# Exponentials written over their tile's scores: one place of two banks each for scores and exponentials becomes two places that hold both

## The chip, the cores and the metric

The kernel runs on one core of one Trainium2 chip. The metric is the device time of one execution in microseconds; lower is better. Five engines matter: TensorE (PE, matrix products, with its weight loads shown as PEld), VectorE (DVE), ScalarE (ACT), GpSimd (POOL) and SyncE (SP, which issues the transfers). Each engine takes its instructions in the order in which the program was written out for it, and waits at an instruction until what that needs is there. The products of PE land in PSUM, eight banks of 2 KB for each of the 128 partitions.

## The reference, cut to what matters

Attention that keeps the 32 largest scores of each row, for 8 batches, 8 heads, 576 positions and 64 columns for each head, and behind it a two-layer network with a rational function between its layers.

```python
def _attn_ref(q, k, v):
    scores = scale * np.matmul(q, k.transpose(0, 1, 3, 2))
    kth = np.partition(scores, -top_k, axis=-1)[..., -top_k:-top_k + 1]
    scores = np.where(scores >= kth, scores, -1000000000.0)
    scores = scores - np.max(scores, axis=-1, keepdims=True)
    attn = np.exp(scores)
    attn = attn / (np.sum(attn, axis=-1, keepdims=True) + 1e-09)
    return np.matmul(attn, v).astype(np.float32)

def _moe_ref(x, w_in, w_out, a, b):
    h = x @ w_in
    h2 = h * h
    h3 = h2 * h
    P = a[0] + a[1] * h + a[2] * h2 + a[3] * h3
    Q = 1.0 + np.abs(b[0]) * np.abs(h) + np.abs(b[1]) * h2
    return ((P / (Q + 1e-06)) @ w_out).astype(np.float32)
```

x has 4608 rows of 512; the hidden layer is 2048 wide.

## The kernel before

**Tiles.** A tile is 128 rows of queries of one head against all 576 keys: 288 tiles, 32 of which hold the 64 left-over rows of two heads (`mixed`). For one tile the steps are, with their lines:

- PE makes the scores (`s`, line 719, or 716 for a mixed tile) in two banks of PSUM; ACT copies them to SBUF (`sb`, 726).
- DVE looks for the 32nd largest score. The 576 columns are three thirds. Four *folds* (745) compare thirds in pairs: the first two take `s` and `sb` and give the smaller and the larger (into `pr`), the other two take `s` and the larger (into `x` and `pr`). Two searches (751) take the eight best of what was folded away. Then four searches for the eight best (762, into `m`) alternate with three *strike-outs* (770) of the eight just found. This is a chain; only the folds and the two searches of 751 have some freedom.
- POOL makes the negative maximum (`st`, 287), ACT the exponentials (`e`, 824), which read `sb` and are written to two other banks of PSUM.
- DVE makes the *masked sum* (827): it compares `sb` with the 32nd value, multiplies with `e`, writes `pr`, and sums.
- PE transposes `pr` (`trp`, 925 and 933), ACT copies the transposes (`p`, 944), and PE multiplies with the values (`av`, 958), for two or four tiles at once and in three parts, on half of the array's columns at a time (128*64 in the trace).

**Hidden layer.** When eight such units have made 256 columns of x (a chunk; 18 in all), PE runs eight groups of hidden products (`ph`, 1116: each of three passes of high and low parts), ACT and POOL the rational function, and PE the output products (`po`, 1311, for the first chunk 1304). The last chunk runs after the last tile. The weights come as float64 and are turned to float32 at the start by ACT, DVE and POOL (512 to 540), and split in high and low parts (565 to 572). The constants of the rational function (`co`, 315 to 430) are worked out on POOL.

**What sets the order.** `add` lists every step with its engine, length, inputs and a due time (`key`); `Plan.run` walks through time and lets each engine take the ready step with the smallest due time, and writes its instructions out there and then. So the order on every engine follows from the table `KEY` (line 21). A `Hold` is a place in a ring (`room`, 223): a step with `take` cannot be chosen while all places of that tag are taken, and the last of the steps with `give` frees it. PSUM's eight banks are: `s` one place of two banks, `e` one place of two banks, `mm` two of one bank (hidden products, transposes, value products), `o` two of one bank (output). Scores hold `s` until the copy and the four folds are through (five users); exponentials hold `e` until the masked sum. `UK` in `KEY` sets how soon the first and the last fold (`f0`, `f3`) come, `AV` how soon the value products come.

Of the kernel before, what the change touches and what calls it, by code (L numbers as in the profile page):

```python
# [20 lines left out]
KEY = {'XM': 1, 'LN': 12, 'UV': 'DVE', 'UK': -883.243, 'B0': ('ACT',), 'B1': ('POOL', 'DVE'), 'B2': ('DVE', 'POOL'), 'B3': ('DVE', 'POOL'), 'WH': ('POOL', 'ACT'), 'XH': ('POOL', 'ACT'), 'TH': 0, 'EU': -3.981, 'HW': 256, 'Q0': ('POOL', 'ACT'), 'Q1': ('POOL',), 'SPLIT': (0, 1, 2, 3, 4, 5, 6, 7), 'XS': 1, 'RH': ('ACT',), 'p2': ('POOL',), 'p4': ('POOL',), 'ratio': ('POOL',), 'ratio_low': ('POOL',), 'URG': -41.622, 'PT': -20.047, 'AV': -43.299, 'MOE': 39.596, 'LOOK': 0.253, 'T': 5.414, 'KL': 0.37, 'PJ': 24.436, 'WL': -1.095, 'EX': 21.72, 'EW': 13.405, 'ALT': {'ACT': 0.627, 'DVE': 84.969, 'POOL': 10.704}, 'WG': 7.127, 'QL': -9.213, 'PACE': 11.13, 'MS': -4.816, 'NM': ('POOL',), 'WD': ('POOL', 'ACT'), 'LP': ('POOL',), 'VL': 2.562, 'VF': 9.72, 'KF': -73.607, 'KG': 4.863, 'PG': 19.476, 'LS': 14.977, 'LG': 7.167, 'PE0': (), 'PO0': 1, 'OK': -24.113, 'OG': 9.815, 'MB': 2, 'KM': 2.703, 'QF': -0.407, 'CUB': (), 'SOFT': 1.0, 'RA': ('POOL', 'ACT'), 'CK': 3.655, 'CO': -111.173, 'CA': -110.941, 'OB': 1, 'CD': 2.11, 'CF': 99.691, 'PL': 0}  # L21
# [15 lines left out]
class Plan:  # L37
# [11 lines left out]
    BACK = 0.17  # L49

    def __init__(self, room):
        self.ring = {t: [-1.0] * n for t, n in room.items()}
        self.left = dict(room)
        self.steps = []
    def fits(self, take):
# [12 lines left out]
    def add(self, eng, length, emit, after=(), key=0.0, take=(), give=(), crit=False, alt=1.0, behind=(), soft=0.0):  # L68
# [8 lines left out]
        s.sig = tuple(sorted(need.items()))  # L77
# [12 lines left out]
        return s  # L90

    def run(self):
# [12 lines left out]
        while left:  # L105
# [9 lines left out]
            while again:  # L115
                again = False
                for e in engines:
# [15 lines left out]
                    again = True  # L133
                    s.end = now + s.length
# [19 lines left out]
    def choose(self, e, ready, soon, now):  # L154
        tops = []
        for sig, q in ready.items():
            while q and q[0][2].end is not None:
                heapq.heappop(q)
            if q:
                tops.append((q[0][0], q[0][1], sig))  # L160
# [22 lines left out]
def tile_topk_attention__then__rational_ffn(  # L183
# [13 lines left out]
    P = 128  # L197
# [272 lines left out]
    def weight_block(name, key, after):  # L470
# [21 lines left out]
        turn, xhold = [] if inner else [Hold("wt")], Hold("mm")  # L492
# [52 lines left out]
        for i in range(len(parts)):  # L545
            s = add("ACT", act_sb(n) + 0.0004 * n, low(i), [ld, s], key + 1,
                    take=([xhold, *hold] if inner else [xhold]) if i == 0 else [])
            d = add("DVE", dve(n), high(i), [s], key + 1)
            signs.append(add("ACT", act_sb(n), sign(i), [d], key + 1))
# [148 lines left out]
    def add_tile(t):  # L698
        t.probs = t.ex = None
        u, kv, key = t.u, t.u.kv, t.key  # L700
        shold = Hold("s", 3 if full or KEY["UV"] == "POOL" else 5)
# [6 lines left out]
        hihold, ehold = Hold("hi") if full else u.xhold, Hold("e")  # L708
# [108 lines left out]
        def exps():  # L817
# [5 lines left out]
            t.e = bank("e", [P, 2, 512], f"e_{t.nm}")[:, :, 0:HF]  # L823
# [21 lines left out]
        else:  # L845
# [12 lines left out]
        ex = add("ACT", act_sb(S, 1), exps, [nm_, u.tiles[0].ex], key + KEY['EX'],  # L858
                 take=[ehold] + (([u.phold, u.uhold] if full else [u.uhold]) if t.h == 0 else []))
# [30 lines left out]
    def add_values(u):  # L890
# [133 lines left out]
        for cs in cuts:  # L1024
            m = add("PE", cold(u.tiles[0].n) * len(cs) * n_av, multiply(cs), [m] if m else pair.ev + [pair.vload], key + KEY['AV'],
                    take=[] if m else [avh] + ([] if u.chunk.parts or u.mixed else [u.chunk.hold]))
# [65 lines left out]
    def add_group(x, o, g, key, split, xs, oholds):  # L1092
# [9 lines left out]
        mm, th = Hold("mm"), {n: Hold("t") for n in ("h", "va", "hh", "pa", "g", "gl")}  # L1102

        def hidden(f, c):
            def emit():
                if f == 0 and c == 0:
                    y.ph = bank("mm", [P, 512], f"ph_{nm}")
# [126 lines left out]
        for f in range(FG):  # L1234
# [11 lines left out]
        if not full:  # L1246
            mm.users = 3
            e1 = add("ACT", act(512, 1), moved, [last, prev.e], ku, give=[mm], take=fours[0:3])
# [122 lines left out]
    def build():  # L1371
# [66 lines left out]
        if not full:  # L1438
# [7 lines left out]
            for _ in range(7):  # L1446
                s = add("POOL", 6 * 0.18, slope_of_root, [s], key=KEY['CD'])
                s = add("DVE", 0.08, turned_slope, [s], key=KEY['CD'])
                s = add("POOL", 0.36, next_root, [s], key=KEY['CD'])
            s = add("POOL", 0.54, near_root, [s], key=KEY['CD'])  # L1450
            for _ in range(2):
                s = add("POOL", 10 * 0.18, slope_near, [s], key=KEY['CD'])
                s = add("DVE", 0.08, turned_slope, [s], key=KEY['CD'])
# [129 lines left out]
```

## Time and profile before

| | us |
|---|---|
| median of 3 runs (1491.86 to 1493.81) | 1493.15 |
| the profiled execution | 1492.21 |
| its span, first to last instruction | 1490.3 |
| PE busy | 1397.2 |
| DVE busy | 1331.9 |
| ACT busy | 1325.9 |
| POOL busy | 1220.5 |

The profile is of one execution. A row of a timeline gives start, length and engine, then line, operation, output<-input, shape and count. A PE instruction's length overlaps the next one's, and a DVE instruction's too by a little, so that the pace of an engine is read from start to start. The span's last 100 us hold no attention.

### The profile page before, as it was taken

The numbers are of one execution on the slowest core, as the hardware profiler recorded it, in microseconds if no ns is written. First come the engines' busy times: TensorE is split into PE (matmuls) and PEld (weight loads), VectorE is DVE, ScalarE is ACT, GpSimd is POOL, SyncE is SP. The second block draws the span as 40 slices with busy tenths as digits, with TensorE's granted clock in tenths as the row PEclk, the third lists the DMA queues.
The fourth block names the chain that finished last, engine by engine and source line by source line (L and its number), as shares of the span: only waits on it lengthen the run. The fifth ranks groups of instructions, "written<-read, shape, count | busy, mean of one in ns | idle before, by whom it ended". The sixth has DMA issues, their size and how long they took to land.

```text
span 1490.3 us, 32446 instructions
## 1 busy us (share of the span) xinstructions
PE 1397.2 (94%) x9793; PEld 1169.7 (78%) x9793; DVE 1331.9 (89%) x5418; ACT 1325.9 (89%) x2440; POOL 1220.5 (82%) x1908
## 2 busy tenths in 40 slices
PE   2657999999999999999999999999999999999997
PEld 1335677888888888888888888888888888888886
DVE  6899999999999999999989998999999999999200
ACT  7898879999898989999899999999899989999785
POOL 8898889779876798779887888779877888777785
PEclk9857999999999999999999999999999999999999
DMA  6764466234533255333533354334533345332333
GB/s 243 254 228 146 135 202 205 86 103 118 165 111 114 89 153 156 90 111 116 172 109 105 98 152 149 103 92 127 173 114 89 118 134 166 89 111 68 100 101 100
DMA packets 110824, 197.25 MB, mean 132 GB/s; under 512 B 15664, under 2 KB 32048, under 8 KB 110640
## 3 DMA queue, kind: packets, MB, share of 16 engines
q1 hardware_dynamic: 110640, 195.08, 43.2%
q8 instruction: 80, 1.31, 0.4%
q14 instruction: 104, 0.85, 0.2%
HBM read 167.78 MB, written 14.68 MB: 122 GB/s over the span
## 4 chain that ended last, share of the span: by engine, by line
PE 72%; ACT 9%; DVE 9%; POOL 5%; DMA 3%; issue 2%; SPq 0%; POOLq 0%; ACTq 0%; DVEq 0%
PE ph_m L1116 19%; PE po_m L1311 17%; PE av L958 9%; PE s L719 7%; PE trp L925 7%; PE po_t L1311 3%; PE ph_t L1116 3%; PE s L716 2%; DVE m L762 2%; DVE pr L827 1%; ACT e L824 1%; PE po_m L1304 1%; DVE pr L745 1%; DVE x L770 1%; DMA w_wo<-in_moe_w_out_dram 1%
## 5 line engine op out<-in xcount | busy, mean ns | idle before, releaser
L1116 PE MATMUL ph_m<-xh_m,win 128*128 128x256 f32 x2048 | 432.9, 289 | 3.7 <-ACT p L944 3.3
L1116 PEld LDWEIGHTS ph_m<-xh_m,win 128*128 128x128 f32 x2048 | 336.8, 188 | 15.3 <-ACT p L944 5.7
L762 DVE MAX8 m<-x 128x8 f32<-128x192 f32 (+1 forms) x864 | 309.4, 358 | 3.8
L1116 PE MATMUL ph_m<-xl_m,win 128*128 128x256 f32 x1024 | 286.1, 279 | 0.0
L925 PE MATMUL trp<-ident,pr 128*128 128x128 f32 x1312 | 226.9, 283 | 38.9 <-ACT wout L535 11.6
L944 ACT COPY p<-trp 128x512 f32<-128x512 f32 (+1 forms) x448 | 229.4, 514 | 22.8 <-PE trp L925 11.6
L719 PE MATMUL s<-k,q 128*128 128x288 f32 x1024 | 201.0, 320 | 37.0 <-DVE x L745 21.6
L827 DVE SCALAR_TENSOR_TENSOR pr<-sb,m,e 128x576 f32<-128x576 f32 x288 | 230.5, 800 | 3.5 <-ACT e L824 2.1
L824 ACT ACTIVATE e<-sb,st 128x576 f32<-128x576 f32 x288 | 217.7, 756 | 17.5 <-POOL st L287 8.6
L925 PEld LDWEIGHTS trp<-ident,pr 128*128 128x128 f32 x1312 | 161.9, 144 | 81.6 <-ACT wout L535 17.8
L745 DVE TENSOR_TENSOR pr<-s,sb 128x192 f32<-128x192 f32 x576 | 198.1, 347 | 25.6 <-ACT sb L726 24.5
L726 ACT COPY sb<-s 128x576 f32<-128x576 f32 x288 | 185.9, 646 | 37.6 <-PE s L719 27.8
L1175 POOL TENSOR_TENSOR pa_m<-pa_m,va_m 128x512 f32<-128x512 f32 x128 | 165.5, 1293 | 54.7 <-ACT va_m L1172 53.4
L719 PEld LDWEIGHTS s<-k,q 128*128 128x128 f32 x1024 | 155.9, 198 | 66.4 <-POOL k L622 10.7
L1311 PE MATMUL po_m<-wout,g_m 128*128 128x512 f32 x480 | 201.9, 421 | 0.0
L751 DVE MAX8 x<-pr 128x8 f32<-128x192 f32 x576 | 199.3, 346 | 0.0
L770 DVE MATCH_REPLACE8 x<-m,x 128x192 f32<-128x192 f32 x576 | 198.3, 344 | 0.0
L1116 PEld LDWEIGHTS ph_m<-xl_m,win 128*128 128x128 f32 x1024 | 193.3, 189 | 3.1 <-issue 0.5
L1311 PE MATMUL po_m<-wl_m,g_m 128*128 128x512 f32 x480 | 189.9, 396 | 1.7 <-DMA wl_m<-wout_l 1.7
L1311 PE MATMUL po_m<-wout,gl_m 128*128 128x512 f32 x480 | 189.4, 395 | 1.9 <-POOL gl_m L1190 1.8
L958 PE MATMUL av<-p,vm 128*64 128x256 f32 (+1 forms) x1920 | 185.2, 341 | 1.6 <-ACT p L944 1.6
L1141 POOL TENSOR_TENSOR pa_m<-pa_m,hh_m 128x512 f32<-128x512 f32 x128 | 165.6, 1294 | 13.7 <-ACT pa_m L1181 4.7
(129 smaller groups left out, 3235.3 us busy)
## 6 DMA issues: line engine op xcount, KB each, us to landing
wl_m<-wout_l SPq DMA_DIRECT2D x240, 256.0 KB, 2.7
vm<-in_v_dram SPq DMA_DIRECT2D x96, 320.0 KB, 3.0
kx<-in_qk_dram SPq DMA_DIRECT2D x64, 288.0 KB, 3.1
qx<-in_qk_dram SPq DMA_DIRECT2D x64, 256.0 KB, 3.0
km<-in_qk_dram SPq DMA_DIRECT2D x32, 352.0 KB, 3.6
w_wo<-in_moe_w_out_dram SPq DMA_DIRECT2D x32, 256.0 KB, 4.8
win<-in_moe_w_in_dram SPq DMA_DIRECT2D x16, 512.0 KB, 5.6
out_dram<-ob_m SPq DMA_DIRECT2D x32, 256.0 KB, 3.4
```

The source lines that it names most:

```text
L719: nc.tensor.matmul(s[:, hf, 0:HF], u.pair.q.q[:, i, t.h, o : o + P], kv.k[:, t.h, cols], start=(i == 0), stop=(i == 1),)
L745: engine().tensor_tensor(out=to, in0=one_, in1=two_, op=op)
L751: nc.vector.max(t.x[:, o : o + 8], t.w[:, 2 * i * TH :][:, 0:TH])
L762: nc.vector.max(t.m[:, 8 * r : 8 * r + 8], src)
L770: nc.vector.match_replace(y, t.m[:, 8 * r : 8 * r + 8], x, NEG)
L824: nc.scalar.activation(t.e, t.sb, AF.Exp, scale=SCALE, bias=t.st)
L827: nc.vector.scalar_tensor_tensor(out=t.pr, in0=t.sb, scalar=t.kth, in1=t.e, op0=ALU.is_ge, op1=ALU.mult, accum_out=u.ss[:, t.h : t.h + 1],)
L925: nc.tensor.transpose(u.ps[i][:, c * P : (c + 1) * P], u.pr[:, x], ident)
L944: nc.scalar.copy(pair.pT[i][:, at].rearrange("p c n -> p (c n)")[:, 0:nw], u.ps[i][:, 0:nw])
L958: nc.tensor.matmul(pair.av[d, 0 : u.nq * len(pair.units)], lhs, x[:, 0, d] if u.mixed else x[:, 0] if lone else x, start=(c == 0), stop=(c ...
L1116: nc.tensor.matmul(y.ph[:, f * nt : (f + 1) * nt], w[c, ff][:, at : at + P], z[:, c, :], start=(c == 0 and i == 0), stop=(c == HP - 1 and ...
L1311: nc.tensor.matmul(o.po[i], z, w, start=(ff == 0 and n == 0), stop=(ff == NF - 1 and n == 2),)
```

## The change

The room for `e` goes, and `s` has two places of two banks. The exponentials of a tile are written over its scores, in the same banks, so a place is held from the scores to the masked sum (six users instead of five), and the exponentials have the four folds among the steps they come after. In a tile's terms: the scores of tile n+1 no longer wait for the folds of tile n, those of tile n+2 wait for the masked sum of tile n.

```diff
     room = KEY.get('ROOM') or {
-        "s": 1, "e": 1, "mm": 2, "o": 2,
+        "s": 2 if KEY["EI"] else 1, "e": 0 if KEY["EI"] else 1, "mm": 2, "o": 2,
...
-        shold = Hold("s", 3 if full or KEY["UV"] == "POOL" else 5)
+        shold = Hold("s", (3 if full or KEY["UV"] == "POOL" else 5) + KEY["EI"])
...
-        hihold, ehold = Hold("hi") if full else u.xhold, Hold("e")
+        hihold, ehold = Hold("hi") if full else u.xhold, shold if KEY["EI"] else Hold("e")
...
-            t.e = bank("e", [P, 2, 512], f"e_{t.nm}")[:, :, 0:HF]
+            t.e = (t.s if KEY["EI"] else bank("e", [P, 2, 512], f"e_{t.nm}"))[:, :, 0:HF]
...
-        ex = add("ACT", act_sb(S, 1), exps, [nm_, u.tiles[0].ex], key + KEY['EX'],
-                 take=[ehold] + (([u.phold, u.uhold] if full else [u.uhold]) if t.h == 0 else []))
+        ex = add("ACT", act_sb(S, 1), exps, [nm_, u.tiles[0].ex] + ([flo] if full else [f0, f2, f3]) * KEY["EI"], key + KEY['EX'],
+                 take=[ehold] * (1 - KEY["EI"]) + (([u.phold, u.uhold] if full else [u.uhold]) if t.h == 0 else []))
```

`KEY` gets `EI` = 1, which switches this on. Five other new entries (`EH`, `JOIN`, `WO`, `SF`, `SC`) are zero and leave the code as it was; a planner's term for leaving the small array shape (`TURN`) counts only with `JOIN` over zero. About thirty numbers of `KEY` are others, among them:

```diff
-'UK': -883.243, 'AV': -43.299, 'MOE': 39.596, 'T': 5.414, 'KF': -73.607, 'KG': 4.863, 'CA': -110.941
+'UK': 15.483, 'AV': 8.05, 'MOE': 14.311, 'T': 4.139, 'KF': -311.617, 'KG': 15.363, 'CA': -206.525
```

So the order changes on all engines. The line numbers of the changed kernel are 9 to 16 higher.

On DVE, in the fifth batch, the steps of the second tile of unit 4_0_2 (names end in a running number; `s_4_0_2_1` is its second tile's scores). Before:

```order
L745 TENSOR_TENSOR pr_4_0_2_11715<-s_4_0_2_1_11747,sb_4_0_2_1_11761 128x192
L762 MAX m_4_0_2_11754<-x_4_0_2_11716 128x8
L745 TENSOR_TENSOR pr_4_0_2_11715<-s_4_0_2_1_11747,sb_4_0_2_1_11761 128x192
L745 TENSOR_TENSOR pr_4_0_2_11715<-s_4_0_2_1_11747,pr_4_0_2_11715 128x192
L770 MATCH_REPLACE x_4_0_2_11716<-m_4_0_2_11754,x_4_0_2_11716 128x192
L745 TENSOR_TENSOR x_4_0_2_11716<-s_4_0_2_1_11747,pr_4_0_2_11715 128x192
L900 RECIPROCAL ss_4_1_1_11646<-ss_4_1_1_11646 128x2
L762 MAX m_4_0_2_11754<-x_4_0_2_11716 128x8
L751 MAX x_4_0_2_11716<-pr_4_0_2_11715 128x8
L770 MATCH_REPLACE pr_4_0_2_11715<-m_4_0_2_11754,x_4_0_2_11716 128x208
L762 MAX m_4_0_2_11754<-x_4_0_2_11716 128x8
L762 MAX m_4_0_2_11754<-pr_4_0_2_11715 128x8
```

After:

```order
L754 TENSOR_TENSOR pr_4_0_2_11559<-s_4_0_2_1_11599,sb_4_0_2_1_11612 128x192
L779 MATCH_REPLACE x_4_0_2_11560<-m_4_0_2_11580,x_4_0_2_11560 128x192
L760 MAX x_4_0_2_11560<-pr_4_0_2_11559 128x8
L754 TENSOR_TENSOR pr_4_0_2_11559<-s_4_0_2_1_11599,pr_4_0_2_11559 128x192
L760 MAX x_4_0_2_11560<-pr_4_0_2_11559 128x8
L771 MAX m_4_0_2_11580<-x_4_0_2_11560 128x8
L754 TENSOR_TENSOR pr_4_1_2_11691<-s_4_1_2_0_11669,sb_4_1_2_0_11682 128x192
L779 MATCH_REPLACE pr_4_0_2_11559<-m_4_0_2_11580,x_4_0_2_11560 128x208
L754 TENSOR_TENSOR x_4_1_2_11692<-s_4_1_2_0_11669,pr_4_1_2_11691 128x192
L771 MAX m_4_0_2_11580<-pr_4_0_2_11559 128x8
L771 MAX m_4_1_2_11711<-x_4_1_2_11692 128x8
L836 SCALAR_TENSOR_TENSOR pr_4_0_2_11559,ss_4_0_2_11622<-sb_4_0_2_1_11612,m_4_0_2_11580,s_4_0_2_1_11599 128x576
```

Before, the tile's folds stand within a few steps of each other, among its searches; now the last fold stands late in the tile, followed at once by its search (760) and by the third search (771), and two tiles overlap less.

On PE, in the same batch, the value product of units 4_0_3 and 4_1_3. Before:

```order
L1311 MATMUL po_m3_2_0_12254<-wl_m3_2_1_1_12308,g_m3_2_1_12283 128x512
L958 MATMUL av_4_1_3_12411<-p0_4_0_3_12192,vm_4_3_0_11877 64x256
L958 MATMUL av_4_1_3_12411<-p1_4_0_3_12223,vm_4_3_0_11877 64x256
L958 MATMUL av_4_1_3_12411<-p0_4_0_3_12192,vm_4_3_0_11877 64x256
L958 MATMUL av_4_1_3_12411<-p1_4_0_3_12223,vm_4_3_0_11877 64x256
L958 MATMUL av_4_1_3_12411<-p0_4_0_3_12192,vm_4_3_0_11877 64x256
L958 MATMUL av_4_1_3_12411<-p1_4_0_3_12223,vm_4_3_0_11877 64x256
L958 MATMUL av_4_1_3_12411<-p0_4_0_3_12192,vm_4_3_0_11877 64x256
L958 MATMUL av_4_1_3_12411<-p1_4_0_3_12223,vm_4_3_0_11877 64x256
L958 MATMUL av_4_1_3_12411<-p2_4_0_3_12252,vm_4_3_0_11877 64x256 x2
L1311 MATMUL po_m3_2_1_12264<-wout3_2218,g_m3_2_1_12283 128x512
```

After:

```order
L1327 MATMUL po_m3_2_0_12083<-wl_m3_2_1_0_12123,g_m3_2_1_12132 128x512
L967 MATMUL av_4_1_3_12217<-p0_4_0_3_12001,vm_4_3_0_11687 64x256
L967 MATMUL av_4_1_3_12217<-p1_4_0_3_12033,vm_4_3_0_11687 64x256
L967 MATMUL av_4_1_3_12217<-p0_4_0_3_12001,vm_4_3_0_11687 64x256
L967 MATMUL av_4_1_3_12217<-p1_4_0_3_12033,vm_4_3_0_11687 64x256
L967 MATMUL av_4_1_3_12217<-p0_4_0_3_12001,vm_4_3_0_11687 64x256
L967 MATMUL av_4_1_3_12217<-p1_4_0_3_12033,vm_4_3_0_11687 64x256
L967 MATMUL av_4_1_3_12217<-p0_4_0_3_12001,vm_4_3_0_11687 64x256
L967 MATMUL av_4_1_3_12217<-p1_4_0_3_12033,vm_4_3_0_11687 64x256
L728 MATMUL s_4_3_0_0_12239<-k_4_0_10013,q_4_0_2_11749 128x288 x4
L967 MATMUL av_4_1_3_12217<-p2_4_0_3_12064,vm_4_3_0_11687 64x256 x2
L1327 MATMUL po_m3_2_1_12110<-wout2_2087,g_m3_2_1_12132 128x512
```

The product stood in one piece between output products; now the next tile's scores stand inside it, so that it is left and entered once more.

On POOL, at the program's start, from its first arithmetic on (`co` are the constants, `q` and `k` queries and keys in high and low parts). Before, the last rows of constants and what follows them:

```order
L321 TENSOR_TENSOR co_74<-co_74 128x1 x5
L324 TENSOR_SCALAR co_74<-co_74 128x1
L321 TENSOR_TENSOR co_74<-co_74 128x1 x3
L324 TENSOR_SCALAR co_74<-co_74 128x1
L321 TENSOR_TENSOR co_74<-co_74 128x1 x3
L667 TENSOR_TENSOR q_0_0_0_135<-qx_0_0_0_105,q_0_0_0_135 128x512
L622 TENSOR_TENSOR k_0_0_139<-kx_0_0_0_107,k_0_0_139 64x576
L622 TENSOR_TENSOR k_0_0_139<-kx_0_0_1_109,k_0_0_139 64x576
```

After, from the first arithmetic on:

```order
L450 MEMSET tiny_79 128x1
L290 TENSOR_SCALAR q_0_0_0_112<-qx_0_0_0_104 128x512
L676 TENSOR_TENSOR q_0_0_0_112<-qx_0_0_0_104,q_0_0_0_112 128x512
L631 TENSOR_TENSOR k_0_0_117<-kx_0_0_0_106,k_0_0_117 64x576
L631 TENSOR_TENSOR k_0_0_117<-kx_0_0_1_108,k_0_0_117 64x576
L676 TENSOR_TENSOR q_0_1_0_125<-qx_0_1_0_110,q_0_1_0_125 128x512
L631 TENSOR_TENSOR k_0_1_140<-kx_0_1_0_115,k_0_1_140 64x576
L631 TENSOR_TENSOR k_0_1_140<-kx_0_1_1_119,k_0_1_140 64x576
```

The constants stood before the first queries and keys; now they stand behind those of the first four pairs of heads.

## Rows read from the trace of the kernel before

**Rows 1.** The page: busy us (share), DVE's busy tenths in 40 slices

```profile
PE 1397.2 (94%) x9793; PEld 1169.7 (78%) x9793; DVE 1331.9 (89%) x5418; ACT 1325.9 (89%) x2440; POOL 1220.5 (82%) x1908
...
DVE  6899999999999999999989998999999999999200
```

**Rows 2.** Stretches: from:to, length, busy us (count) PE, PEld, DVE, ACT, POOL, clock, DMA

```profile
100.00:150.00 50.00, 32.66 (x172) 23.93 (x173) 48.36 (x188) 43.49 (x84) 43.50 (x80) 0.73 0.50 163
...
900.00:950.00 50.00, 49.95 (x377) 43.75 (x378) 45.04 (x179) 47.60 (x88) 41.01 (x58) 1.00 0.44 134
...
1400.00:1450.00 50.00, 49.50 (x319) 44.23 (x318) 0.00 (x0) 39.92 (x64) 40.10 (x36) 1.00 0.35 106
```

**Rows 3.** Timeline of DVE: start, us; folds of tiles 49 and 281, masked sums

```profile
266.53 0.35 DVE L745 TENSOR_TENSOR pr<-s,sb 128x192 f32<-128x192 f32 x1
...
799.72 0.80 DVE L827 SCALAR_TENSOR_TENSOR pr<-sb,m,e 128x576 f32<-128x576 f32 x1
...
804.16 0.80 DVE L827 SCALAR_TENSOR_TENSOR pr<-sb,m,e 128x576 f32<-128x576 f32 x1
...
1348.63 0.35 DVE L745 TENSOR_TENSOR pr<-s,sb 128x192 f32<-128x192 f32 x1
```

**Rows 4.** Timeline of DVE near 57 us: strike-outs and what follows them

```profile
54.79 0.09 DVE L770 MATCH_VALUE_LOAD x<-m,x 128x8 f32 x1
...
55.12 0.35 DVE L745 TENSOR_TENSOR x<-s,pr 128x192 f32<-128x192 f32 x1
...
58.70 0.09 DVE L770 MATCH_VALUE_LOAD x<-m,x 128x8 f32 x1
...
59.15 0.38 DVE L762 MAX8 m<-x 128x8 f32<-128x208 f32 x1
```

**Rows 5.** Timeline of PE around one value product

```profile
813.02 0.39 PE L1311 MATMUL po_m<-wout,gl_m 128*128 128x512 f32 x1
813.25 0.40 PE L1311 MATMUL po_m<-wl_m,g_m 128*128 128x512 f32 x1
813.58 2.38 PE L958 MATMUL av<-p,vm 128*64 128x256 f32 x20
815.89 0.50 PE L1311 MATMUL po_m<-wout,g_m 128*128 128x512 f32 x1
816.23 0.39 PE L1311 MATMUL po_m<-wout,gl_m 128*128 128x512 f32 x1
```

**Rows 6.** Timeline of the first 13 us: POOL, ACT, PE, DVE

```profile
3.20 0.19 POOL L321 TENSOR_TENSOR co<-co 128x2 f32<-128x2 f32 x1 [1.27 <-DVE co L328]
...
7.87 1.26 POOL L667 TENSOR_TENSOR q<-qx,q 128x512 fp32r<-128x512 f32 x1
9.21 2.77 POOL L622 TENSOR_TENSOR k<-kx,k 64x576 fp32r<-64x576 f32 x2
...
3.96 0.63 ACT L279 ACTIVATE q<-qx 128x512 fp32r<-128x512 f32 x1 [1.25 <-DMA qx<-in_qk_dram]
5.22 1.46 ACT L279 ACTIVATE k<-kx 128x576 fp32r<-128x576 f32 x2 [0.63 <-DMA kx<-in_qk_dram]
...
10.66 1.33 PE L719 MATMUL s<-k,q 128*128 128x288 f32 x4 [10.66 <-POOL k L622]
...
12.70 0.62 DVE L745 TENSOR_TENSOR pr<-s,sb 128x192 f32<-128x192 f32 x2 [9.59 <-ACT sb L726]
```

**Rows 7.** Waits from 0 to 250 us: who waited for whom, us, times, longest

```profile
PE s L719 <- DVE x L745: 19.9, 13, 3.9
...
DVE pr L745 <- ACT sb L726: 14.9, 13, 9.6
```

**Rows 8.** Timeline near 168 us: scores, copy, first fold

```profile
168.17 0.77 PE L719 MATMUL s<-k,q 128*128 128x288 f32 x4
...
168.97 0.65 ACT L726 COPY sb<-s 128x576 f32<-128x576 f32 x1
...
169.66 0.36 DVE L745 TENSOR_TENSOR pr<-s,sb 128x192 f32<-128x192 f32 x1 [0.84 <-ACT sb L726]
```

**Rows 9.** The page's groups: the exponential, busy us, mean ns, idle before

```profile
L824 ACT ACTIVATE e<-sb,st 128x576 f32<-128x576 f32 x288 | 217.7, 756 | 17.5 <-POOL st L287 8.6 <-DVE pr L827 7.5 <-DVE x L770 0.4
```

More of the change, by code (lines that the diff above doesn't have):

```diff
@@ L49 @@
     BACK = 0.17
+    TURN = 0.24
     def __init__(self, room):
         self.ring = {t: [-1.0] * n for t, n in room.items()}
-        self.left = dict(room)
+        self.left = dict(room, tiled=1)
         self.steps = []
+        self.tiled = False
     def fits(self, take):
@@ L66, in grab, with add @@
         self.left[h.tag] -= 1
-    def add(self, eng, length, emit, after=(), key=0.0, take=(), give=(), crit=False, alt=1.0, behind=(), soft=0.0):
+    def add(self, eng, length, emit, after=(), key=0.0, take=(), give=(), crit=False, alt=1.0, behind=(), soft=0.0, tiled=False):
         s = Obj()
@@ L133, in run @@
                     again = True
+                    if e == "PE":
+                        s.length += self.TURN if self.tiled and not s.tiled else 0.0
+                        self.tiled = s.tiled
                     s.end = now + s.length
@@ L159, in choose @@
             if q:
-                tops.append((q[0][0], q[0][1], sig))
+                keep = KEY['JOIN'] if e == "PE" and self.tiled and q[0][2].tiled else 0.0
+                tops.append((q[0][0] - keep, q[0][1], sig))
         tops.sort()
@@ L491, in weight_block @@
         hold = [Hold("wl")] if inner else [Hold("t") for _ in range(2)]
-        turn, xhold = [] if inner else [Hold("wt")], Hold("mm")
+        turn, xhold = [] if inner else [Hold("wt")], Hold("o" if KEY["WO"] and (inner or name[1] < KEY["WO"]) else "mm")
         parts = [slice(0, 512)] if inner else [slice(0, 256), slice(256, 512)]
@@ L547, in weight_block @@
                     take=([xhold, *hold] if inner else [xhold]) if i == 0 else [])
-            d = add("DVE", dve(n), high(i), [s], key + 1)
+            d = add("DVE", dve(n), high(i), [s], key + 1, soft=KEY["SF"])
             signs.append(add("ACT", act_sb(n), sign(i), [d], key + 1))
@@ L1025, in add_values @@
             m = add("PE", cold(u.tiles[0].n) * len(cs) * n_av, multiply(cs), [m] if m else pair.ev + [pair.vload], key + KEY['AV'],
-                    take=[] if m else [avh] + ([] if u.chunk.parts or u.mixed else [u.chunk.hold]))
+                    take=[] if m else [avh] + ([] if u.chunk.parts or u.mixed else [u.chunk.hold]), tiled=KEY['JOIN'] > 0)
         m.give = [pair.vhold] + [thold[0]] + ([] if u.mixed else [thold[1]])
@@ L1101, in add_group @@
         y.late = x.n >= KEY['LN']
-        mm, th = Hold("mm"), {n: Hold("t") for n in ("h", "va", "hh", "pa", "g", "gl")}
+        y.early = x.opening and g < KEY['EH']
+        mm, th = Hold("o" if y.early else "mm"), {n: Hold("t") for n in ("h", "va", "hh", "pa", "g", "gl")}
         def hidden(f, c):
@@ L1106, in emit @@
                 if f == 0 and c == 0:
[L1107 removed]
+                    y.ph = bank(mm, [P, 512], f"ph_{nm}")
                 ff, at = (g * FG + f) // 4, (g * FG + f) % 4 * P
@@ L1233, in add_group @@
                 wdep += w_steps.get(("o", g * FG + f), [])
-        for f in range(FG):
+        if y.early:
+            for c in range(HP):
+                for f in range(FG):
+                    last = add("PE", 3 * pe_r(nt), hidden(f, c),
+                               [split[c // 2], last, prev.ph] + w_steps.get(("i", c, (g * FG + f) // 4), []), key,
+                               take=[mm] if last is None else [], give=[xs] if f == FG - 1 and c == HP - 1 else [])
+        for f in range(0 if y.early else FG):
             for c in range(HP):
@@ L1247, in add_group @@
             mm.users = 3
-            e1 = add("ACT", act(512, 1), moved, [last, prev.e], ku, give=[mm], take=fours[0:3])
+            e1 = add("ACT", act(512, 1), moved, [last, prev.e] + params * y.early, ku, give=[mm], take=fours[0:3])
             s1 = add("ACT", act(512, 1), rooted, [e1], ku + 0.1, give=[mm])
@@ L1452, in build @@
                 s = add("POOL", 10 * 0.18, slope_near, [s], key=KEY['CD'])
-                s = add("DVE", 0.08, turned_slope, [s], key=KEY['CD'])
+                s = add("DVE", 0.08, turned_slope, [s], key=KEY['CD'], soft=KEY["SC"])
                 s = add("POOL", 0.36, nearer, [s], key=KEY['CD'])
```

8 lines of the change are left out of this document (5 added, 3 removed).

## Prediction

> **What bounds the kernel now.** I read the page first, then the fifty-microsecond stretches, then the orders of the two engines that are full, then their single rows. The page shows TensorE (PE) busy 94% of 1490.3 us and VectorE (DVE) 89%, with the DVE's last four slices nearly empty [rows 1]. The stretches show three stages [rows 2]. At the start (100 to 150 us) the DVE is busy 48.4 of 50 us and PE only 32.7: the weights are still being prepared, and there is little hidden-layer work to give to PE. In the middle both are near 50 (900 to 950: PE 49.95, DVE 45.0). From 1400 on the DVE is idle and PE runs hidden-layer work alone. So the start costs what the DVE needs, the end what PE needs, and the middle whichever of the two has more to do in each short stretch.
>
> I checked that last sentence by counting. A tile takes 15 DVE steps; where none waits, one tile's masked sum follows the other's after 4.44 us [rows 3]. From the order before I took, for each eight tiles, the DVE's steps at their start-to-start times and PE's products at theirs, and kept the larger of the two. Over the 232 tiles from number 49 to number 280 this gives 1065 us (DVE alone 1048, PE alone 1051). The trace has 1082.1 for them, from the first fold at 266.53 to the one at 1348.63 [rows 3]. So 17 us of the middle are waits that the count lacks. The first 48 tiles count 240 us and take 253.8, from 12.70 [rows 6] to 266.53: 14 us of waits. What stands behind number 280 on PE counts 132 us.
>
> **The change, part by part.** The first part is the two places. A tile's exponentials now overwrite its scores; the place comes free only after the masked sum (line 827), not after the folds (line 745), but there are two places in turn. The operations and their sizes are the same. The exponential now waits for all four folds of its tile. What is large is that the planner's numbers changed with it, so that nearly every engine's order is another one. I cost that from the two orders.
>
> *DVE.* In the order before, two tiles are woven together, and a step seldom stands right behind the one whose result it needs. Where it does, it starts later: the second strike-out is followed by the third search of the same tile after 0.45 us (58.70 to 59.15), while a strike-out that is followed by another tile's fold frees the engine after 0.33 (54.79 to 55.12) [rows 4]. That is 0.12 us for each pair. In tiles 49 to 280 such pairs number 174 before and 380 after: 206 more, 206 x 0.12 = 25 us, so that the DVE's middle grows from 1048 to 1073. The new pairs are mostly kinds that do not occur before (last fold to its search, that search to the third search: 250 in the middle). Their price I bound by 0, if such pairs are free, and 0.2, somewhat above the row; I take the row's 0.12, since they have the same form, a step that reads what the step just before it wrote.
>
> *PE.* The product with the values (line 958) uses another shape of the array, 128x64, and each entry and exit costs. Between output products the step is 0.23 us (813.02 to 813.25); into the product it is 0.33 (813.25 to 813.58), the product's 20 records take 2.31 instead of 20 x 0.108 = 2.16 that its single records show one after another, and the first output product behind it takes 0.34 (815.89 to 816.23) [rows 5]. Together 0.10 + 0.15 + 0.11, or 0.34 us by the middle of all such episodes. Before, each product stood in one piece: 96 episodes. Now its three parts often stand apart with scores or transposes between them: 142. In the middle it is 118 against 76, so 42 x 0.34 = 14 us. Besides, about 9 us of hidden-layer work move into the middle, 6 from the start and 3 from the end. PE's middle goes from 1051 to 1075.
>
> *Both.* With both engines' new counts the larger of the two over eight tiles sums to 1084.5 in the middle, 19.5 more than before. The first 48 tiles count 241.1 against 239.9, the end 128.6 against 131.8. The sum of the count is +17.5 us.
>
> *The start of the start.* Before, GpSimd works on the polynomial's constants from 3.20 us, and only at 7.87 turns to the low part of the first queries; the keys' low part follows at 9.21, and the first scores start at 10.66 behind it [rows 6]. The keys' high parts were there from ScalarE well before (5.22 to 6.7). After, the constants' load and their arithmetic stand behind the first four pairs' queries and keys, and GpSimd makes the first query's high part itself. By these rows: queries landed by 3.96, high part 0.62, low part 1.26, keys' low part 1.4, the first scores at about 7. I credit 3.7 us. The constants are wanted only by the first hidden group, near 130 us, so their delay should cost nothing; if that cover is gone, it costs what the group waits.
>
> *The waits.* In the first 250 us PE waits 19.9 us for the folds to free the one place, but PE has time there; what counts is that the DVE waits 14.9 us for copies of scores, of which 9.6 is the very first (priced above) [rows 6, 7]. The rest, 5 us, is what the second place can take. In the middle such waits are short. I credit 3 us in all.
>
> *The added waits.* From scores to the copy and on to the first fold took 168.17 to 169.66, 1.5 us, with the DVE standing for 0.84 of it [rows 8]; with the signal before it about 1.7. In the new order the time between a masked sum and the first fold two tiles on is 1.7 us at least and 2.5 in the middle; in the old one the time between a tile's last fold and the next tile's first was 1.8 and 2.7. So the chain still fits, with a little less room. Behind the exponential, which now waits for the folds, ScalarE holds the next tile's copy and the transposes' copies; from the last fold to the masked sum lie 2.3 us, the exponential itself is 0.76 of them [rows 9]. I price both at zero, with 0 and 0.1 us for each tile as bounds.
>
> **Sum** for the profiled execution, 1492.2 us with a span of 1490.3 (0.9 under the median of the runs shown): 1492.2 + 17.5 - 3.7 - 3 = 1503.
>
> **A rule against it.** Rows 4 show that a step right behind the one it depends on starts 0.12 us later than an independent one. The Trainium skill, page "VectorE: DVE Perf Modes", section "The DRAIN you can't avoid", says that the engine empties its pipe after every operation whether or not the next one waits, and that a semaphore after each "costs nothing extra". By it the DVE's new order would be free, and the case below is what it would give; the rows disagree for the pairs that they show.
>
> **The rivals.**
> *Dependent pairs of the new kinds are free.* Then the larger of the two sums to 1444.5 against 1436.7, +8, because PE's 14 us remain: 1492.2 + 8 - 6.7 = 1493.5, no change. For it: no such pair is in the trace. Against it: all kinds that are show the delay.
> *The second place takes the waits out.* The count lacks 14 us at the start and 17 in the middle, 31 in all. If the second place removes 22 of them instead of 3, the result is 1503 - 19 = 1484, faster. It decides from 10 us of waits removed. For it: scores can be made a tile earlier, and PE's single waits of the middle are mostly before scores and transposes. Against it: the place is held longer, so that the chain's room hardly grows, and now both engines are equally full in almost every stretch, where before one mostly had room.
> *The longer hold becomes the bound.* The scores stand in PE's order behind pieces of up to a microsecond, and the chain needs 1.7 of 1.7 to 2.5 us. If each of the 288 tiles is 0.1 us late, that is 29 us: 1532. It decides wherever scores start over half a microsecond after their place is free.
>
> **How the numbers follow.** Forecast near 1503: 0.47. Free pairs, about 1493.5: 0.1. Waits removed, about 1484: 0.28. Longer hold, about 1532: 0.15. The unknown pair price moves the forecast by -10 (free) to +14 (0.2 each, which the count gives as 1469 in place of 1454), its own range 1494 to 1517. The range reaches down past the waits case by the 4 us by which its 22 are a guess, and up a little over the forecast's own end: 1480 to 1520, which leaves out most of the hold case and the rest of the waits. About 0.2% of the time, 3 us, is what a measurement of this kernel tells from no change. Faster: the waits case and a little of the free pairs, 0.3. Same: most of the free pairs and the forecast's lowest end, 0.12. Slower: 0.58.
>
> **What would show it.** Dependent pairs on the DVE: last fold to search and on to the third search, 0.38 us or so instead of 0.26. PE episodes of the value product: 142, each about 0.34 us of entry and exit. First scores near 7 us. The 232 middle tiles at 1090 to 1105 us instead of 1082, the work behind the DVE's end some 3 us shorter. The forecast is wrong if the middle takes 1080 or less, which means that the waits were worth more than the count, or over 1115, which the hold would do, seen as the DVE's idle time before the first fold.

## The result, and the profile after

The changed kernel takes 1515.3 us in the median of four runs (1514.23 to 1516.39) against 1493.1 for the kernel before: a ratio of 1.0146, with an interval of 1.0133 to 1.0158. That is 22 us slower. The forecast was slower by 10 (1503); the time lies within the range, but the loss is twice the one forecast. The signs that the prediction named came: 0.38 us from the last fold to its search, 142 episodes, first scores at 7.11 us, and 1104.9 us for the middle (1090 to 1105 forecast). The profiled execution took 1514.8 us with a span of 1513.0.

The page of the changed kernel, in the form of [rows 1], busy us and the busy tenths of the DVE:

```profile
span 1513.0 us, 32281 instructions
PE 1409.6 (93%) x9793; PEld 1168.5 (77%) x9793; DVE 1358.7 (90%) x5418; ACT 1332.0 (88%) x2431; POOL 1227.9 (81%) x1917
DVE   6899999999999999999999999999999999999300
```

The stretches from the first fold to that of tile 49, from there to that of tile 281, and to the end (columns: from:to, length, busy us and count of PE, PEld, DVE, ACT and POOL, granted clock, DMA share, GB/s). First the kernel before:

```profile
12.70:266.53 253.83, 189.12 (x1157) 137.28 (x1157) 240.27 (x944) 217.94 (x424) 226.72 (x436) 0.87 0.59 195
266.53:1348.63 1082.10, 1074.02 (x7784) 916.89 (x7782) 1050.96 (x4311) 992.32 (x1820) 882.52 (x1331) 1.00 0.41 121
1348.63:1490.30 141.67, 132.68 (x854) 114.55 (x852) 40.34 (x164) 108.97 (x183) 101.94 (x109) 0.99 0.31 93
```

Then the changed kernel:

```profile
9.14:269.84 260.70, 181.98 (x1114) 131.24 (x1113) 243.82 (x950) 214.96 (x423) 225.43 (x451) 0.83 0.58 192
269.84:1374.74 1104.90, 1096.12 (x7850) 924.62 (x7849) 1074.87 (x4311) 1006.33 (x1828) 895.68 (x1343) 1.00 0.41 120
1374.74:1513.00 138.26, 129.50 (x829) 111.07 (x828) 40.01 (x160) 106.82 (x177) 100.27 (x108) 0.99 0.31 91
```

So the whole difference of 22.7 us in the span is -3.6 before the first fold, +6.9 in the first 48 tiles, +22.8 in the middle and -3.4 behind it. In the middle both engines grew by about the same, PE by 22.1 us of busy time and DVE by 23.9, and both are almost always busy. Which of the two made the time longer cannot be read from busy time; the experiments have to tell.

**The DVE's account.** For each step of the DVE in the middle I took the time from its start to the next one's, and split the sum in three: the usual time of an independent step of that kind, what dependent neighbours took above that, and what is left, the waits. The usual times add up to 1027 us in every kernel whose steps are the same. The last column is the whole middle. In e3, e5 and e7 the steps stand in the same order as without the edit, but 237 of the pairs (214 in e7) read other columns, so that the second step no longer needs the first.

| kernel | dependent pairs | their extra | waits | middle |
|---|---|---|---|---|
| before | 174 | 23.5 | 31.4 | 1082.1 |
| changed | 380 | 48.4 | 29.3 | 1104.9 |
| e3, pairs freed | 380 in place | 17.8 | 58.8 | 1103.9 |
| e4, less PE work | 380 | 48.2 | 17.9 | 1093.4 |
| e5, both | 380 in place | 17.7 | 43.1 | 1088.1 |
| e6, products joined | 487 | 63.8 | 16.2 | 1107.0 |
| e7, joined and freed | 487 in place | 35.3 | 38.7 | 1100.9 |
| e1, old numbers | 679 | 84.6 | 38.4 | 1149.9 |
| e2, old structure | 763 | 100.3 | 27.7 | 1155.3 |

The forecast's price of a pair stands: 206 pairs more are 24.9 us more, 0.12 each. The timeline of the DVE in the changed kernel shows the two new kinds in a row (start, length, then what it did):

```profile
890.35 0.34 DVE L760 MAX8 x<-pr 128x8 f32<-128x192 f32 x1
890.60 0.34 DVE L754 TENSOR_TENSOR pr<-s,pr 128x192 f32<-128x192 f32 x1
890.98 0.36 DVE L760 MAX8 x<-pr 128x8 f32<-128x192 f32 x1
891.38 0.38 DVE L771 MAX8 m<-x 128x8 f32<-128x208 f32 x1
```

The search at 890.35 is followed after 0.25 us by a fold that does not need it. The search of what that fold gave starts 0.38 behind it, the third search, which needs both, 0.40 behind that.

**PE's account.** The hidden layer's products in the middle, before and after (line 1116, in the changed kernel 1126: hidden products; line 1311, then 1327: output products). Before, each kind in its fence; the columns are from:to, length, busy us and count, clock, DMA:

```profile
266.53:1348.63 1082.10, 385.83 (x2718) 1.00 0.41 121
...
266.53:1348.63 1082.10, 377.68 (x1360) 1.00 0.41 121
```

After:

```profile
269.84:1374.74 1104.90, 387.90 (x2764) 1.00 0.41 120
...
269.84:1374.74 1104.90, 378.14 (x1380) 1.00 0.41 120
```

46 hidden products more at 0.118 us and 20 output products more at 0.231 are 10 us of work that came into the middle. The value product is the other part: 1520 records as before, but 118 episodes in place of 76. From the first record of an episode to the first record behind it they took 138.2 us before and 145.7 now, 7.5 more. The step into an episode and the first step behind it are longer than the usual step, in sum by 7.7 and 7.9 us before and by 11.2 and 12.3 now. Together that is 15.4 us more, or 0.37 for each new episode. One of them in the changed kernel, on PE, scores between its two pieces:

```profile
827.03 0.40 PE L1327 MATMUL po_m<-wl_m,g_m 128*128 128x512 f32 x1
827.35 1.95 PE L967 MATMUL av<-p,vm 128*64 128x256 f32 x16
829.23 0.80 PE L728 MATMUL s<-k,q 128*128 128x288 f32 x4
829.96 0.65 PE L967 MATMUL av<-p,vm 128*64 128x256 f32 x4
830.54 0.50 PE L1327 MATMUL po_m<-wout,g_m 128*128 128x512 f32 x1
830.87 0.40 PE L1327 MATMUL po_m<-wout,gl_m 128*128 128x512 f32 x1
```

10 and 15.4 are 25.5 us of new work on PE. What is left of PE's middle, waits and steps slower than usual, is 30.1 us before and 27.3 now; the two changes together are the 22.8. So each engine alone has enough new work for the whole loss.

### The profile page after: what moved, and what is told of

It is laid out like the page before. It is cut to its first block, busy times and chain, and to the rows that moved or that the text cites. A ratio compares the mean times of both kernels' runs of the same rounds, so it can differ in the third digit from the quotient of the medians.

```text
span 1513.0 us, 32281 instructions
## 1 busy us (share of the span) xinstructions
PE 1409.6 (93%) x9793; PEld 1168.5 (77%) x9793; DVE 1358.7 (90%) x5418; ACT 1332.0 (88%) x2431; POOL 1227.9 (81%) x1917
## 4 chain that ended last, share of the span: by engine, by line
PE 75%; DVE 9%; ACT 9%; POOL 3%; DMA 2%; issue 2%; SPq 0%; POOLq 0%; ACTq 0%; DVEq 0%
PE ph_m L1126 21%; PE po_m L1327 19%; PE av L967 10%; PE trp L934 8%; PE s L728 7%; PE ph_t L1126 3%; PE po_t L1327 3%; DVE m L771 2%; PE s L725 2%; DVE pr L836 2%; DVE pr L754 2%; ACT p L953 2%; ACT s L833 1%; DVE x L779 1%; PE po_m L1320 1%
## 5 line engine op out<-in xcount | busy, mean ns | idle before, releaser
L1126 PEld LDWEIGHTS ph_m<-xh_m,win 128*128 128x128 f32 x2048 | 336.4, 189 | 17.8 <-ACT p L953 6.7
L728 PE MATMUL s<-k,q 128*128 128x288 f32 x1024 | 206.7, 326 | 48.5 <-DVE pr L836 41.2
L836 DVE SCALAR_TENSOR_TENSOR pr<-sb,m,s 128x576 f32<-128x576 f32 x288 | 231.2, 803 | 1.6
L833 ACT ACTIVATE s<-sb,st 128x576 f32<-128x576 f32 x288 | 217.6, 755 | 14.2 <-DVE pr L754 5.5
L754 DVE TENSOR_TENSOR pr<-s,sb 128x192 f32<-128x192 f32 x576 | 199.2, 346 | 26.9 <-ACT sb L735 23.9
L967 PE MATMUL av<-p,vm 128*64 128x256 f32 (+1 forms) x1920 | 192.6, 340 | 3.6 <-ACT p L953 2.3
```

Source lines behind the costliest of these rows:

```text
L728: nc.tensor.matmul(s[:, hf, 0:HF], u.pair.q.q[:, i, t.h, o : o + P], kv.k[:, t.h, cols], start=(i == 0), stop=(i == 1),)
L754: engine().tensor_tensor(out=to, in0=one_, in1=two_, op=op)
L833: nc.scalar.activation(t.e, t.sb, AF.Exp, scale=SCALE, bias=t.st)
L836: nc.vector.scalar_tensor_tensor(out=t.pr, in0=t.sb, scalar=t.kth, in1=t.e, op0=ALU.is_ge, op1=ALU.mult, accum_out=u.ss[:, t.h : t.h + 1],)
L967: nc.tensor.matmul(pair.av[d, 0 : u.nq * len(pair.units)], lhs, x[:, 0, d] if u.mixed else x[:, 0] if lone else x, start=(c == 0), stop=(c ...
L1126: nc.tensor.matmul(y.ph[:, f * nt : (f + 1) * nt], w[c, ff][:, at : at + P], z[:, c, :], start=(c == 0 and i == 0), stop=(c == HP - 1 and ...
```

## Experiments

**e1 and e2: the two halves of the change.** The structure with the old numbers, and the new numbers with the old structure.

```diff
e1: KEY of before, with 'EI': 1
e2: KEY of after, with 'EI': 0
```

> The changed structure (two places, exponentials over the scores, held to the masked sum) with all the planner's numbers of before. Theory A, the place's longer hold makes the plan put dependent DVE steps side by side: 679 dependent pairs in tiles 49 to 280 against 174 before and 380 after, at the 0.12 us measured, so the DVE's middle is 1108 us by the count and the time near 1540 (1492 + 50). Theory B, the retuned numbers make the pairs and the structure itself costs nothing: near 1492. Theory C, the pieces of the value product cost the time: here it stands in one piece (96 episodes), so 1500 or less.

> The structure of before (one place for scores, one for exponentials) with the numbers of after. Theory A: the numbers were fitted to the two places; with one place the count has 763 dependent pairs in the middle, so about 1550. Theory B, the numbers alone explain the loss: near 1515. If the two places were a cost by themselves and the numbers were not, near 1493.

Measured: 1573.0 us (ratio 1.0531, 1.0512 to 1.0550) and 1573.2 (1.0533, 1.0513 to 1.0553). Theory A's direction is right in both, and its counts of 1540 and 1550 are too low by 33 and 23 us. Each half alone costs 80 us, and the other half wins 58 of them back: numbers and structure are fitted to each other. With the old numbers and the places held to the masked sum the plan puts more dependent steps side by side, 679 pairs instead of 174. What the two places would cost under the numbers that suit them best, no run shows. And the hold itself binds here, as the third rival had it: PE's waits over the whole of e1 (who waited for whom, us, times, longest) are

```profile
PE s L728 <- DVE pr L836: 61.1, 23, 10.8
PE trp L934 <- DVE pr L836: 15.4, 18, 2.8
```

of which 21.7 and 15.0 us fall in the middle. In the changed kernel the first of them is 2.1 us in the middle. So the new numbers bought the hold's waits off. That they did it with value products in pieces has some support in e7 below; that the late folds do it is not shown.

**e3: the pairs' extra taken away, the order kept.** Two searches read other columns, so that they need not wait for the step before them.

```diff
-nc.vector.max(t.x[:, o : o + 8], t.w[:, 2 * i * TH :][:, 0:TH])
+nc.vector.max(t.x[:, o : o + 8], t.w[:, 0:TH])
...
-src = t.x[:, 0:TH] if r < 2 else t.x if r == 2 else t.w[:, 0:XW]
+src = t.x[:, 0:TH] if r < 2 else t.x[:, 0 : TH + 8] if r == 2 else t.w[:, 0:XW]
```

> The changed kernel, same order on every engine, but the search behind the last fold reads the first fold's result again, and the third search reads 200 columns and so not that search's result: these two steps no longer need the one just before them (the computed threshold is then that of other candidates). 269 or so dependent pairs lose their 0.12 us. If the DVE alone sets the start and the middle: 32 us less, 1483. If the larger of DVE and PE in each stretch does: 9 us less, 1506, because PE is as full. If neither (waits on the place set it): within 2 us of 1515.

Measured: 1513.8 us (ratio 1.0145, 1.0125 to 1.0166), 1.5 below the changed kernel, where the larger of the two had 9 less. The extra did go: the same three steps in its timeline now follow after 0.26 and 0.27 us.

```profile
888.29 0.34 DVE L754 TENSOR_TENSOR pr<-s,pr 128x192 f32<-128x192 f32 x1
888.55 0.35 DVE L760 MAX8 x<-pr 128x8 f32<-128x192 f32 x1
888.82 0.35 DVE L771 MAX8 m<-x 128x8 f32<-128x200 f32 x1
```

Over the middle 30.6 us of extra went and 29.5 us of waits came. The first folds' waits for the copy of the scores, in the middle of the changed kernel and then of e3:

```profile
DVE pr L754 <- ACT sb L735: 8.3, 23, 1.2
```

```profile
DVE pr L754 <- ACT sb L735: 28.7, 76, 1.2
```

The copy waits for the scores, and the scores for their turn on PE, which itself waits for next to nothing there (1.7 us for places). So it came out where the third theory had it, but not by waits on the place. With PE's new work in place, the pairs cost next to nothing: 1.0 us of the middle.

**e4 and e5: less PE work, and both reliefs.** One of the five key chunks is left out of the value products; in e5 together with e3's edits.

```diff
-                    for h in range(2):
+                    for h in range(0 if c == 2 else 2):
```

> The changed kernel with one of the five key chunks left out of the value products (some 31 us of PE work over the whole, in the same places of the order). If the DVE alone sets the middle: 2 us less or no change (1513 to 1515), PE only waits more. If the larger of the two does: about 10 us less, 1505. If PE alone does: 26 to 31 us less, 1486.

> The two edits of the runs with freed pairs and with less PE work together: same order, searches that do not need the step before them, and one key chunk of the value products left out. If the changed kernel's middle goes by whichever engine has more to do, each relief alone is held up by the other engine, and both together give more than their sum (1.5 + 16): by the count 35 us less, 1480. If something else holds it up once one engine has room (scores' place kept to the masked sum), the sum at most: 1497 or more.

Measured: 1499.1 us (ratio 1.0042, 1.0028 to 1.0056) and 1493.1 (1.0013, 1.0001 to 1.0025). In the middle the chunk is 23 us of PE (from the first record of an episode to the first behind it, 122.8 in all instead of 145.7). 11.5 us of the middle came back in e4 and 16.8 in e5. So the pairs, worth 1.0 alone, are worth 5.3 once PE has room. The sum of the two reliefs is 12.5, both together give 16.8: the engines cover for each other, but less sharply than the larger of the two would have it. By the count e4 was to gain 10 us in all and e5 35; they gained 16 and 22. The whole of e5 came out 13 us above its 1480.

**e6 and e7: the pieces joined again.** The planner is told to stay with the value product once it is in it, and with that it also counts a time for leaving it (`TURN`); e7 with e3's edits.

```diff
-'JOIN': 0.0
+'JOIN': 60.0
```

> The changed kernel with the planner told to keep the three pieces of a value product together: 96 episodes instead of 142, PE's middle 1053 instead of 1075 by the count; but scores come later, and dependent DVE pairs in the middle rise from 380 to 494, the DVE's middle from 1073 to 1087, its start by 6. If PE alone sets the middle: 22 less there, 9 more at the start, 3 less at the end, 1499. If the larger of the two: 11 more, 1526. If neither: 1515.

> The run with the value products kept in one piece, and in it the searches that do not need the step before them (as in the run with freed pairs, whose 1513.8 it is to be compared with). Both have DVE room; PE has 46 episodes of the value product less. If these episodes' 0.34 us are on the path: by the count 1443 against 1445.5 in all, with 22 less PE in the middle and 9 more at the start; with PE as what sets the middle, 1513.8 - 22 + 5 = 1497. If they are covered: 1514 or, with the longer start, 1520.

Measured: 1527.1 us (ratio 1.0234, 1.0217 to 1.0251), and 1520.0 (1.0189, 1.0172 to 1.0206). The larger of the two had 1526 for e6, but that it fits is luck: of the 14 us that it gave the DVE's middle 2.1 came, and the first 48 tiles took 12.1 more, not 6. Neither run shows the episodes' price by itself: with 22 us less on PE the middle of e7 is 3 us shorter than that of e3. The plan changed with it. The pieces had let scores in early; with whole products PE reaches the next transposes or scores before the masked sum is done. In the middle of e7 PE waits

```profile
PE trp L934 <- DVE pr L836: 4.0, 5, 2.7
PE s L728 <- DVE pr L836: 3.6, 7, 0.9
```

where e3 has 0.5 and 1.7, and the first 48 tiles are 13 us longer. Joining them is no repair.

**e9 and e10: more switches in the kernel before.** 160 useless transposes, behind each value product or between its pieces; the order is kept. They are written to free columns of the scores' banks. First e9's edit, then e10's:

```diff
+                if NJ in cs:
+                    for _ in cuts[1:]:
+                        nc.tensor.transpose(prev.bank[:, 0, HF : HF + P], ident, ident)
```

```diff
+                else:
+                    nc.tensor.transpose(prev.bank[:, 0, HF : HF + P], ident, ident)
```

> The kernel before, same order on every engine, with one or two useless 128x128 transposes (160 in all, 0.11 us each) put right behind each value product. The control for the run with the split products. If PE sets the middle and the end: 128 in the middle and 6 behind it, 15 us more, 1507. If the DVE sets them: 1493.

> The kernel before, same order on every engine, with the same 160 transposes put between the pieces of each value product, so that it is left and entered again 160 times more (128 in the middle). Nothing else differs from the run with the transposes behind. If an episode's 0.34 us are on the path wherever PE is full: 0.34 x 130 = 44 us above the control, about 1551. If the larger of the two engines counts and DVE covers a part: 25 to 40 above. If the episodes are covered by waits: less than 5 above.

Measured: 1526.6 us (ratio 1.0232, 1.0215 to 1.0249) and 1556.0 (1.0429, 1.0411 to 1.0446). The control is 35 us slower, not 15: since the transposes stand in the scores' banks, the program makes folds wait for them with semaphores of its own (38 folds in e9, 85 in e10, none in the kernel before). The DVE's waits over the whole of e9, and of e10:

```profile
DVE pr L745 <- PE s L965: 17.0, 20, 2.6
DVE x L745 <- PE s L965: 12.7, 20, 1.2
```

```profile
DVE pr L745 <- PE s L954: 29.5, 55, 2.3
...
DVE x L745 <- PE s L954: 8.3, 24, 0.7
```

That spoils the control, and a part of the difference: the folds' waits are 29.7 us in the one and 37.8 in the other. 160 episodes more went with 29 us more, 0.18 each, where an episode takes 0.37 on PE in the changed kernel. That is in favour of the episodes being felt in part; it does not settle how much.

**e11: the start's numbers of before.**

```diff
-'KF': -311.617, 'KG': 15.363, 'CA': -206.525
+'KF': -73.607, 'KG': 4.863, 'CA': -110.941
```

(with `KL`, `CO`, `CD` and `CF` likewise.)

> The changed kernel with the numbers of before for the keys of the first batch and for the constants, so that the constants stand ahead again. First fold at 12.6 us instead of 9.1. If the earlier first scores are worth their 3.6 us: the count gives the first 48 tiles 4 more, PE's middle 7 less (1068), the end 1.4 more, so 1515 + 3.6 + 4 - 7 + 1 = 1517. If the constants' own steps only moved into the first 48 tiles and took the gain back: those tiles 2.5 us shorter, 1512 or less.

Measured: 1526.7 us (ratio 1.0230, 1.0213 to 1.0247). The first fold comes at 12.58 us, 3.4 later, and the first 48 tiles take 263.0, 2.3 more (81 pairs in place of 67). So the early scores are a true gain, and the constants' steps did not take it back. The rest of the loss is in the middle (+4.4), where the order is another one too.

**e12: more DVE work in the kernel before.** One short search more in each tile, its result unread.

```diff
                 nc.vector.max(t.m[:, 8 * r : 8 * r + 8], src)
+                if r == 3:
+                    nc.vector.max(t.m[:, 40:48], t.m[:, 0:24])
```

> The kernel before, same order, with one more short DVE step in each tile (a search over 24 columns whose result nobody reads, about 0.1 us by its size against the 0.26 of one over 192), that is some 23 us more DVE work in the middle, about what the changed kernel's dependent pairs add there, and 5 in the first 48 tiles. If the larger of the two engines in each eight tiles counts, as in the prediction: 4 at the start and 15 in the middle, 1512. If PE alone sets the middle of the kernel before and the DVE's idle time takes the steps up: 5 at the start and at most 5 in the middle, 1497 to 1502. If the DVE sets it: 28 more, 1521.

Measured: 1504.4 us (ratio 1.0069, 1.0053 to 1.0086). In the middle the steps are 23.4 us; 4.2 of pairs' extra went, since the new step stands between some, and 10.2 of waits. 9.1 us remained, between the 15 of the larger of the two and the 5 of PE alone. In the kernel before neither engine alone sets the middle: 19 us more on the DVE cost 9.

**e8: another way to have two places.** Not a test of the forecast, but a try at something better: two places of scores that are free after the folds, with the exponentials in SBUF, where the probabilities will stand.

```diff
-t.e = (t.s if KEY["EI"] else bank("e", [P, 2, 512], f"e_{t.nm}"))[:, :, 0:HF]
+t.e = t.s[:, :, 0:HF] if KEY["EI"] == 1 else t.pr
```

> Another structure with the numbers of before: two places for scores that are free again after the folds, and the exponentials written into the probabilities' place in the large memory, where the masked sum then works in place (the third strike-out gets a place of its own). It has the second place without the longer hold. Dependent pairs in the middle 126 (before 174), PE's middle 1062 (before 1051), count 1440 against 1437. If a second place takes no waits out: 1495. If it takes out 20 of the 31 us of waits: 1475. If the masked sum or the exponential is slower on these places (0.1 us for each of 288 tiles): 1520.

Measured: 1592.5 us (ratio 1.0677, 1.0659 to 1.0695). The price of the masked sum, which I had put at 0.1 us at most, decides. The groups of the DVE, first of the changed kernel, then of e8 (busy us, mean ns, idle before):

```profile
L836 DVE SCALAR_TENSOR_TENSOR pr<-sb,m,s 128x576 f32<-128x576 f32 x288 | 231.2, 803 | 1.6
```

```profile
L838 DVE SCALAR_TENSOR_TENSOR pr<-sb,m,pr 128x576 f32<-128x576 f32 x288 | 309.1, 1074 | 1.2 <-DVE m L771 0.2
```

0.27 us for each of 288 tiles are 78 of the 101 us that e8 lost; the rest was not followed.

None of the twelve is faster than the kernel before.

## Why the prediction was right in its direction and short in its size

The step that failed is the count by the larger of the two engines, most of all in its term for the first 48 tiles: +1.2 us in the sum, +6.9 measured. Beside it stands the credit of 3 us for waits, of which nothing came. The experiments show the same of the rule itself: it had 9 us less for e3, 35 less for e5 and 15 more in e12's middle, and 1.5 less, 22 less and 9.1 more came.

- **Dependent pairs on the DVE: +25 us of DVE time.** Right to the tenth: 24.9, at 0.12 for each. The new kinds, of which the trace of before had none, cost 0.11 and 0.13. The rival that they are free is dead (0.38 against 0.26). With it goes, for steps of this form, the sentence of the Trainium skill ("VectorE: DVE Perf Modes", "The DRAIN you can't avoid") that a semaphore after each operation costs nothing extra. The same section also says that a next operation that is not held starts earlier, so that it does not make all steps equal. But e3 shows that in the changed kernel 31 us of this cost 1 us of the middle. Most of it was covered.
- **PE: +14 for the episodes, +9 of hidden layer.** Right in number (142 episodes; 118 in the middle) and nearly in size: 15.4 and 10. e4 shows that about half of PE's work is felt, 11.5 of 23 us, and 15.8 of 23 with the pairs gone (e3 against e5).
- **The larger of the two: +19.5 in the middle.** It measured 22.8. The rule is too sharp. By an estimate from e12 (9.1 for 19) the pairs alone would be worth some 12 us. PE's new work, with the order that comes with it, is worth most of 22: e3 has all of it and less of the pairs' extra than the kernel before (17.8 against 23.5), and stands 21.8 above it. Both together are the 22.8. What the rule missed is that the time above the count is no constant: 17 us before and 20 now (1104.9 against 1084.5), and when both engines were relieved in e5 the whole stood 13 us further above the count. The DVE's waits stand where PE is late, and grow when the DVE alone gets less to do (29.3 to 58.8 in e3).
- **The first 48 tiles: +1.2.** This is the term that was mis-sized most; it measured +6.9. By the DVE's account 3.1 are pairs (67 in place of 44), 1.1 other steps and 2.7 waits, above all the reciprocals' for GpSimd. The prediction itself says that the start costs what the DVE needs, and the DVE's steps alone are 4.2 of the 6.9. Its count let PE's lighter load in tiles 33 to 40 (busy 42.7 us before, 39.2 now) give 2.5 us back. The trace gave 1.3 there, and took 3.6 and 3.9 in the eight tiles before and behind; PE's load had moved on into tiles 41 to 48 (34.4 to 38.3). A part of the waits may be the granted clock, which is 0.83 in this stretch of the profiled execution and 0.87 before. In tiles 25 to 32 it is 0.92, and they took 41.3 us; e3, with 1.00 there, took 38.6, and the kernel before, with 0.95, 37.7. But the other three executions of the changed kernel, with 0.977 and 0.978 over the whole where the profiled one has 0.969, took no less time (1514.2 to 1516.4 us against 1514.8), while in e3 the two executions with 0.968 took 3.3 us more than the two with 0.978. How much of the 6.9 us is the clock stays open. The DVE's waits for the reciprocals in this stretch, before and then now, and those for the copies of the scores:

```profile
DVE ss L900 <- POOL ss L281: 1.1, 4, 0.5
```

```profile
DVE pr L754 <- ACT sb L735: 15.6, 11, 9.1
DVE ss L909 <- POOL ss L290: 3.4, 5, 1.3
```

- **The start of the start: -3.7.** First scores at 7.11 us, forecast near 7; the first fold 3.6 earlier. Right, and e11 gives it back. The rows that answer to [rows 6]:

```profile
3.62 0.62 POOL L290 TENSOR_SCALAR q<-qx 128x512 fp32r<-128x512 f32 x1 [1.69 <-DMA qx<-in_qk_dram]
...
5.66 2.80 POOL L631 TENSOR_TENSOR k<-kx,k 64x576 fp32r<-64x576 f32 x2
...
7.11 2.73 PE L728 MATMUL s<-k,q 128*128 128x288 f32 x8 [7.11 <-POOL k L631]
```

- **The end: -3.2.** It measured -3.4.
- **The waits: -3.** Nothing came. The DVE's waits for copies in the first 48 tiles, without the very first, are 6.5 us now (15.6 less 9.1) and were 5.3 (14.9 less 9.6, [rows 7]). All waits rose by 2.7 there and fell by 2.1 in the middle. The second place took no waits out, which is the answer to the rival at 1484.
- **The hold at zero.** Right for the changed kernel (2.1 us of PE's waits for places in the middle), by the grace of its numbers; e1 shows what it costs without them. The signal that its chain puts at about 0.2 us is shorter: the scores start as little as 0.06 us behind the masked sum that frees their place.

So the 11.8 us between the sum and the profiled execution are 5.7 of the first 48 tiles, 3.3 of the middle and 3 of waits credited that did not come, less 0.2 at the two ends. How far the episodes alone, apart from the order that comes with them, would go into the time stays open: e7 and e10 do not settle it.

## What to carry to other kernels

Where two engines are both nearly full, price the new work of each, and take neither their sum nor a clean maximum: one's waits stand where the other is late, and do not shrink because a count of work says that there is room. A relief on one of them alone is no measure of what its work costs; relieve the other too. And a longer hold of a place shows first in the order, as steps that stand beside what they need, before any wait for the place can be seen.

## What was not expected of the hardware

With both its operands in SBUF the masked sum took 1074 ns instead of 803, and GpSimd's little scaling of one column beside it grew as well, before and then in e8:

```profile
L287 POOL TENSOR_SCALAR st<-m 128x1 f32<-128x1 f32 x288 | 55.2, 192 | 37.1 <-DVE m L762 33.8
```

```profile
L296 POOL TENSOR_SCALAR st<-m 128x1 f32<-128x1 f32 x288 | 113.6, 395 | 38.9 <-DVE m L771 35.1
```

Both engines lose. The Trainium skill, "SBUF — State Buffer", section "SBUF: two separate sides", says that a DVE operation with two SBUF inputs and a GpSimd operation that reads SBUF exclude each other for a whole instruction. The trace of e8 agrees: the 150 scalings that met no masked sum took 191 ns in the mean, the 138 that ran beside one 617, while in the changed kernel, with one operand in PSUM, it is 191 and 192. The masked sums of e8 took 803 ns in the five cases in which GpSimd was idle throughout, and 1084 in the 192 in which it was busy throughout.
